# A transform and gated-MLP block: the last block of G kept on the chip, chunks ahead of products in the second, and one w_sp sum made in the last stage

## Chip, cores and metric

The kernel runs on one core of a Trainium2 chip. The metric is the device time of one execution in microseconds (us); the median of several executions is compared. All data are fp32 in DRAM at the start and the end.

## What is computed

```python
h = layernorm(x) * (1 + ca) + sa                        # x: [2048, 512]
x = x + ga * Re(DFT_seq(DFT_hid(h)))                    # Cr @ (h Wr') - Ci @ (h Wi')
h = layernorm(x) * (1 + cb) + sb
z = gelu(h @ w_in)                                      # [2048, 1792]
z1, z2 = z[:, :896], layernorm(z[:, 896:])
g = w_sp @ z2 + b_sp                                    # w_sp: [2048, 2048]
x = x + gb * ((z1 * g) @ w_out)
```

The six vectors sa, ca, ga, sb, cb, gb are silu(c) @ w_mod, cut into six pieces of 512; the text calls them vectors 0 to 5. Cr and Ci are the real and imaginary DFT matrices of the sequence (2048 x 2048), Wr and Wi those of the hidden axis. The kernel multiplies in the other order: first the sequence (G, from Cr, Ci and h), then the hidden axis (y, from G and Wr, Wi).

## The kernel before

**Products.** Each fp32 product is made as three matmuls of a reduced fp32 type: every operand is split into a high part (`hi`, a copy on ACT) and a rest (`lo`, a subtraction on DVE), and `matmul3` (L95) issues hi·hi, hi·lo and lo·hi. So for each block that PE multiplies, ACT makes one pass and DVE one or two (a transpose, and the rest).

**Slots and the order.** The program is one list of slots, each about 12 matmuls [128x128]·[128x512], and every other instruction is put at a slot by hand: `atd(n, f, ...)` runs `f` after the matmuls of slot n have been issued. All queues are in order: PE, ACT, DVE, POOL (stores, and small operations of the norms) and SP (loads). An instruction that waits holds back all that stands behind it on its engine.

**G stage, slots 0 to 121.** G is made in four row blocks of 512 rows.
- The first (t = 0) takes 32 slots (`mm_a`, L636) and all eight PSUM banks. While it runs, `load_first` (L572) loads four blocks of Cr and Ci for the products of t = 1 (roles 21, 11, 12, 22) and `turn_s` transposes them.
- Blocks t = 1, 2, 3 take 30 slots each, o..o+29 with o = 32, 62, 92: 14 slots of `s` units (`mm_s`, seven products of a Strassen-like scheme over sums of Cr and Ci blocks that `sum_f` makes, in the order 1, 5, 6, 2, 7, 3, 4), then 16 slots of `k` units (`mm_k`, plain chunks of Cr and Ci, two slots each). For every unit `turn_unit` transposes a chunk on DVE (the `k` units), `hi_unit` copies on ACT and `lo_unit` subtracts on DVE, two or three units ahead of its matmuls. After products 1, 5, 6 and 7 ACT copies PSUM banks (`mm_s`).
- Chunks come through a `stage` ring of two buffers: when one has been transposed, `block_done` loads the next but one.
- `out_k` (L708) stores the G of a block in DRAM (`g_d`): two ACT copies, two DVE sums and four stores of 256 KB a half.

**Modulation.** Vectors 2, 3, 4 are made by `load_mod`, `sum_mod` (four weighted sums on DVE), `split_mod`, and `spread_mod` (two matmuls with a matrix of ones). Vectors 0, 1 and 5 are made as columns: for each of four pieces a transpose (L184) and a product (L336) on DVE and a sum on ACT. Vector 5 then goes through DRAM (`store_mod`, `read_mod`).

**w_sp sums.** The spatial product, too, is made of products over sums of w_sp's quadrants. Four sums are made ahead of it: `load_s` loads four pieces of 128 x 512 (two loads of 512 KB), `sum_s` makes two sums on DVE in each of two calls and POOL stores them (`s_d`, four stores of 256 KB). There are 16 such sets (r, g, b), five in the G and y stages, eleven in z1.

**y stage, slots 122 to 153.** For each of 16 tiles of 128 rows: `load_g` (512 KB from `g_d`, two buffers), `split_g`, `seed_y` (ACT puts x into a PSUM bank), two slots of `mm_y` (j = 0, 1: real, imaginary), then `post_y` (ACT copy, store, statistics on DVE and POOL), `norm_y` (ACT) and `post_h` (two DVE operations, a store of h2).

**Then** come z1 (N2, h2 read back, loads `stage<-h_d`, the first half of w_in), z2, the spatial product gw (N4) and the output product.

Of the kernel before, what the change touches and what calls it, by code (L numbers as in the profile page):

```python
# [19 lines left out]
def fnet_gmlp_kernel(  # L20
# [531 lines left out]
    order_b = {}
    for t in range(1, NQ):
        more = t < NQ - 1
        names = ([("s", t + 1, 21), ("s", t + 1, 11), ("s", t + 1, 12)] if more else []) + \
            [("k", t, 0), ("k", t, 1), ("k", t, 2)] + ([("s", t + 1, 22)] if more else []) + [("k", t, 3)]
        for k in names:
            order_b[k] = 8 + len(order_b)
# [1009 lines left out]
```

## Time and profile before

| | us |
|---|---|
| runs before | 958.56, 960.98, 962.49 |
| median | 960.98 |
| profiled execution | 963.18 |
| its span, first to last instruction | 961.4 |
| granted TensorE clock, mean | 0.993 |

The profile gives times of the one profiled execution; 1.8 us of it lie outside the span. A stretch is found again by the stages: row block 0 of G until about 100 us, blocks 1 to 3 from 100.5, 184.6 and 270.5, y from 354, z1 from 449, z2 from 528, gw from 617, the output product from 905 us. PE runs the same kind of matmul nearly all the time, so a stretch in which PE waits shows as one with fewer matmuls.

### The profile page before, as it was taken

The page shows a single profiled execution, that of the slowest core. Times are in us where ns is not written, and L with a number is a line of the kernel's source. Part 1 is how long each engine was busy: PE and PEld are TensorE (multiplying, and loading weights), DVE is VectorE, ACT ScalarE, POOL GpSimd, SP SyncE. Part 2 cuts the span into 40 slices and gives each one's busy share as a digit, 9 for nine tenths or more (in the row PEclk, how much of TensorE's full clock was granted, in tenths as well). Part 3 has the DMA queues.
Part 4 walks back from the last instruction along what each step waited for, and adds up shares of the span by engine and source line. Part 5 has one row for each costly group of instructions (what it writes and reads, how often), then busy time and mean ns, then how long its engine had stood idle before and what let it go on. Part 6 is the DMA issues. An engine that isn't in the chain of part 4 may idle for free.

```text
span 961.4 us, 12161 instructions
## 1 busy us (share of the span) xinstructions
PE 932.5 (97%) x4086; PEld 769.7 (80%) x4086; DVE 747.7 (78%) x1021; ACT 434.7 (45%) x694; POOL 165.5 (17%) x333
## 2 busy tenths in 40 slices
PE   9989999999999998999979999999999999999998
PEld 6768887887878886787758999888888888888886
DVE  7789787998779864978767678888688679785882
ACT  3584543452254353554638355635544344432221
POOL 1330000100120113753333255400000000000000
PEclk9999999999999999999989999999999999999999
DMA  9997299759955739995996789664555355833541
GB/s 205 221 230 163 95 205 205 175 160 234 228 122 120 231 120 314 319 268 177 271 339 246 240 243 281 186 160 117 141 127 121 88 132 126 213 90 120 202 156 59
DMA packets 273743, 179.10 MB, mean 186 GB/s; under 512 B 135376, under 2 KB 240080, under 8 KB 273552
## 3 DMA queue, kind: packets, MB, share of 16 engines
q1 hardware_dynamic: 257136, 131.90, 57.1%
q0 software_dynamic: 13552, 43.81, 11.9%
q10 hardware_dynamic: 2992, 2.62, 1.1%
q8 instruction: 32, 0.52, 0.2%
q14 instruction: 31, 0.25, 0.1%
HBM read 133.17 MB, written 45.10 MB: 185 GB/s over the span
## 4 chain that ended last, share of the span: by engine, by line
PE 65%; DMA 11%; issue 9%; DVE 8%; POOL 4%; SPq 3%; ACT 1%; ACTq 0%; POOLq 0%; DVEq 0%
PE gw L98 9%; PE gw L99 9%; PE gw L97 9%; PE z2p L98 3%; PE z2p L97 3%; PE z2p L99 3%; PE op L97 3%; PE op L98 3%; PE op L99 3%; SPq L162 2%; DMA stage<-in_A_dft_seq_im_dram 2%; PE gs_c L98 2%; PE gs_c L97 2%; PE gs_c L99 2%; PE gp L98 2%
## 5 line engine op out<-in xcount | busy, mean ns | idle before, releaser
L98 PE MATMUL gw<-al,bh 128*128 128x512 f32 x400 | 155.9, 390 | 0.8 <-DVE al L270 0.8
L97 PE MATMUL gw<-ah,bh 128*128 128x512 f32 x400 | 155.6, 389 | 0.0
L99 PE MATMUL gw<-ah,bl 128*128 128x512 f32 x400 | 155.6, 389 | 0.0
L270 DVE TENSOR_TENSOR al<-t,ah 128x512 fp32r<-128x512 f32 x136 | 92.6, 686 | 60.2 <-PE gw L98 44.8
L263 ACT ACTIVATE ah<-t 128x512 fp32r<-128x512 f32 x136 | 84.7, 625 | 101.3 <-PE gw L99 56.1
L98 PEld LDWEIGHTS gw<-al,bh 128*128 128x128 f32 x400 | 75.1, 188 | 17.0 <-DVE al L270 1.6
L97 PEld LDWEIGHTS gw<-ah,bh 128*128 128x128 f32 x400 | 75.1, 188 | 15.8
L99 PEld LDWEIGHTS gw<-ah,bl 128*128 128x128 f32 x400 | 75.1, 188 | 15.5
L228 DVE STREAM_TRANSPOSE t<-stage 128x1024 f32<-128x1024 f32 x56 | 69.4, 1239 | 0.0
L1049 ACT ACTIVATE bh<-z 128x512 fp32r<-128x512 f32 (+1 forms) x56 | 32.8, 586 | 62.3 <-PE gw L98 62.3
L619 DVE TENSOR_TENSOR pl<-f,ph 128x1024 fp32r<-128x1024 f32 x42 | 50.8, 1212 | 12.8 <-ACT ph L615 12.6
L615 ACT ACTIVATE ph<-f 128x1024 fp32r<-128x1024 f32 x42 | 44.3, 1057 | 30.9 <-PE gs_c L99 8.9
L543 DVE STREAM_TRANSPOSE tp<-stage 128x1024 f32<-128x1024 f32 x36 | 44.5, 1235 | 16.9 <-DMA stage<-in_A_dft_seq_im_dram 11.5
L98 PE MATMUL gs_c<-pl,hh 128*128 128x512 f32 x144 | 56.2, 390 | 0.6 <-DVE pl L619 0.6
L97 PE MATMUL yp<-hth,gh 128*128 128x512 f32 x128 | 51.0, 398 | 5.3 <-ACT yp L812 5.3
L99 PE MATMUL gs_c<-ph,hl 128*128 128x512 f32 x144 | 56.1, 389 | 0.0
L97 PE MATMUL gs_c<-ph,hh 128*128 128x512 f32 x144 | 56.0, 389 | 0.0
L615 ACT ACTIVATE ph<-tp 128x1024 fp32r<-128x1024 f32 x35 | 36.9, 1054 | 37.2 <-DVE tp L543 16.6
L1027 POOL DMA_DIRECT2D s_d<-sj x64 | 35.4, 553 | 104.1 <-DVE sj L1019 53.4
L99 PE MATMUL yp<-hth,gl 128*128 128x512 f32 x128 | 50.6, 395 | 0.0
L98 PE MATMUL yp<-htl,gh 128*128 128x512 f32 x128 | 50.5, 394 | 0.0
L98 PE MATMUL z2p<-wil,ah 128*128 128x448 f32 x128 | 46.7, 365 | 0.0
(270 smaller groups left out, 2227.7 us busy)
## 6 DMA issues: line engine op xcount, KB each, us to landing
sj<-in_B_w_sp_dram SPq DMA_DIRECT2D x32, 512.0 KB, 7.0
s_d<-sj POOLq DMA_DIRECT2D x64, 256.0 KB, 5.5
stage<-s_d SPq DMA_DIRECT2D x128, 128.0 KB, 2.9
stage<-in_A_dft_seq_re_dram SPq DMA_DIRECT2D x52, 256.0 KB, 5.6
stage<-in_A_dft_seq_im_dram SPq DMA_DIRECT2D x52, 256.0 KB, 6.6
stage<-in_B_w_sp_dram SPq DMA_DIRECT2D x96, 128.0 KB, 3.2
gr<-g_d SPq DMA_DIRECT2D x16, 512.0 KB, 7.3
stage<-h_d SPq DMA_DIRECT2D x32, 256.0 KB, 6.6
```

The source lines that it names most:

```text
L97: nc.tensor.matmul(acc, ah, bh, start=first, stop=False, skip_group_check=go_on)
L98: nc.tensor.matmul(acc, ah, bl, start=False, stop=False, skip_group_check=go_on)
L99: nc.tensor.matmul(acc, al, bh, start=False, stop=last, skip_group_check=go_on)
L162: engs[q % len(engs)].dma_start(tile_[32 * q:32 * q + 32, :, s0:s1], v[q][:, :, s0:s1])
L228: nc.vector.transpose(t.rearrange("p r (b i) -> p r b i", i=32), st[:, :, :, 16 * k:16 * k + 32])
L263: nc.scalar.activation(AH[n], source(n), AF.Copy)
L270: nc.vector.tensor_tensor(AL[n], source(n), AH[n].bitcast(F32), op=ALU.subtract)
L543: nc.vector.transpose(dst.rearrange("p k (b i) -> p k b i", i=32), st[:, :, 64 * m:64 * m + 64].rearrange("p b (k i) -> p k b i", k=2))
L615: nc.scalar.activation(pair_of(PH, u, "ph"), source_unit(u), AF.Copy)
L619: nc.vector.tensor_tensor(pair_of(PL, u, "pl"), source_unit(u), PH[u].bitcast(F32), op=ALU.subtract)
L1027: nc.gpsimd.dma_start(s_d[m, r, g][b * P:(b + 1) * P, :], a)
L1049: nc.scalar.activation(BH[p, k][:, :w], b_of(p, k), AF.Copy)
```

## The change

- **Last row block of G.** `out_last` takes the place of `out_k` for t = 3: hi and lo of G are made from PSUM into SBUF tiles (ACT copies, DVE sums and subtractions), and `g_d[3]` is neither stored nor loaded. The y stage takes the tiles of this block first (order `YORD`), j = 0 for its four tiles and then j = 1; so these four end in successive slots. The buffers `gh` and `gl` become one ring of five. z1 takes the row blocks in the same order (`TS`).
- **Second row block (t = 1).** Four chunks (8 slots) come ahead of the products; `keep_p` copies their four banks to `UM[1]`. After products 1 and 5 DVE subtracts these from PSUM where ACT copied. The loads and transposes of the first `s` blocks, and the sums 5 and 7, come later.
- **Modulation.** Vector 5 is made like 2, 3, 4, ACT copying it from PSUM. The columns of 1 and 0 move from t = 1 to t = 2. Vectors 2, 4 and 3 are made earlier. `turn_ht` of the real part moves eight slots ahead.
- **w_sp sums.** A set is three pieces and three sums. The fourth, `sum_s4`, is made in gw from a quadrant of w_sp and the second sum: eight times two loads of 512 KB, one DVE subtraction [128x1024] and a store of 512 KB. The sets are placed anew: five in G, the others from YE+14.

```diff
+    TS = (NQ - 1, *range(NQ - 1))
     src = [quad((cr, ci)[j], 0, g) for g in range(NQ) for j in range(2)]
+    CHUNKS = {1: (("k", 1, 0), ("k", 1, 1), ("s", 2, 21), ("s", 2, 11), ("s", 2, 12), ("k", 1, 2), ("k", 1, 3), ("s", 2, 22)),
+              2: (("s", 3, 21), ("s", 3, 11), ("s", 3, 12), ("k", 2, 0), ("k", 2, 1), ("k", 2, 2), ("s", 3, 22), ("k", 2, 3)),
+              3: (("k", 3, 0), ("k", 3, 1), ("k", 3, 2), ("k", 3, 3))}
+    order_b = {}
     for t in range(1, NQ):
-        if t < NQ - 1:
-            src += [quad(cr, t + 1, 3), quad(cr, t + 1, 2), quad(ci, t + 1, 2)]
-        src += [quad(cr, t, 0), quad(cr, t, 1), quad(ci, t, 0)]
-        if t < NQ - 1:
-            src.append(quad(ci, t + 1, 3))
-        src.append(quad(ci, t, 1))
+        for kind, t_, i in CHUNKS[t]:
+            order_b[kind, t_, i] = len(src)
+            src.append(quad((cr, ci)[i // 2], t_, i % 2) if kind == "k" else
...
+        if j == 5:
+            mods[5] = cpool.tile([P, D], F32, tag="mod5", bufs=1, name="mod5")
+            nc.scalar.activation(mods[5], ps, AF.Copy)
+            return
...
+        first = 4 if t == 1 else 0
+        units += [("k", t, i) for i in range(first)] + [("s", t, i) for i in range(14)] + \
+            [("k", t, i) for i in range(first, 8)]
...
-        return {"c11": 0, "u": 2 if t % 2 else 4, "v": 4 if t % 2 else 2, "c22": 6}[role]
+        return {"c11": 0, "u": 2 if t == 3 else 4, "v": 4 if t == 3 else 2, "c22": 6}[role]
...
+                if t == 1:
+                    nc.vector.tensor_tensor(C["u", f], C["c11", f], UM[t][:, f, :], op=ALU.subtract)
+                else:
+                    nc.scalar.activation(C["u", f], C["c11", f], AF.Copy)
...
+                um = UM[t][:, 2 + f, :]
+                if t == 1:
+                    nc.vector.tensor_tensor(um, C["v", f], um, op=ALU.subtract)
+                else:
+                    nc.scalar.activation(um, C["v", f], AF.Copy)
...
+    def keep_p():
+
+        for f in range(2):
+            nc.scalar.activation(UM[1][:, f, :], C["c11", f], AF.Copy)
+        for f in range(2):
+            nc.scalar.activation(UM[1][:, 2 + f, :], C["v", f], AF.Copy)
...
+        if fresh and s == 7:
+            UM[t] = outs.tile([P, 4, D], F32, tag="um", bufs=1, name=f"um{t}")
+            keep_p()
...
+    def ring(name, dtype=F32R):
+        return yp[0].tile([P, 2, D], dtype, tag="gt", bufs=5, name=name)
+
+    def out_last(j):
+
+        def lo(dst, src, hi):
+            nc.vector.tensor_tensor(dst, src, hi.bitcast(F32), op=ALU.subtract)
+
+        t = NQ - 1
+        um = UM[t][:, 2 * j:2 * j + 2, :]
+        if j == 0:
+            hs, ls = [[ring(f"gt{m}0"), None] for m in "hl"]
+        else:
+            both_ = [blocks.tile([P, 4, D], F32R, tag="stage", bufs=2, name=f"gt{m}1") for m in "hl"]
+            hs, ls = [[b[:, 2 * e:2 * e + 2, :] for e in range(2)] for b in both_]
+        for f in range(2):
+            nc.scalar.activation(hs[0][:, f, :], C["u" if j else "c11", f], AF.Copy)
+        for f in range(2):
+            nc.vector.tensor_tensor(um[:, f, :], C["c22" if j else "v", f], um[:, f, :], op=ALU.add)
+        for f in range(2):
+            lo(ls[0][:, f, :], C["u" if j else "c11", f], hs[0][:, f, :])
+        if j == 0:
+            hs[1], ls[1] = [ring(f"gt{m}1") for m in "hl"]
+        nc.scalar.activation(hs[1], um, AF.Copy)
+        lo(ls[1], um, hs[1])
+        for e in range(2):
+            for f in range(2):
+                GT[4 * j + 2 * e + f] = hs[e][:, f, :], ls[e][:, f, :]
...
-        YP[m] = bank(4 + m % 4, f"yp{m}")
+        i = YORD.index(m)
+        YP[m] = bank((0, 1, 4, 5)[i] if i < 4 else (6, 7, 4, 5)[i % 4], f"yp{m}")
         nc.scalar.activation(YP[m], X.pop(("r", m)), AF.Copy)
...
+            gh, gl = [g[:, m % 4 * P:m % 4 * P + P] for g in GT[c_]] if m // 4 == NQ - 1 else \
+                (GH[m][:, c_, :], GL[m][:, c_, :])
+            matmul3(YP[m], gh, gl, ht_hi[j, k], ht_lo[j, k], False, c_ == 7, True)
...
+        nc.sync.dma_start(t[:, 0], w_sp[o:o + P, g * Q:(g + 1) * Q])
+        v = w_sp.rearrange("r (j c) -> r j c", j=2)[S // 2 + o:S // 2 + o + P]
+        nc.sync.dma_start(t[:, 1:], v[:, :, g * Q:(g + 1) * Q])
...
-            nc.vector.tensor_tensor(a12, a12, a11, op=ALU.subtract)
-            done = (2, a11), (4, a12)
+            done = (2, a11),
...
+    def load_s4(r, g, h):
+
+        t = S4[r, g, h] = spre[-1].tile([P, 2, 2, Q], F32, tag="hz", bufs=2, name=f"s4_{r}{g}{h}")
+        rows_ = slice(2 * h * P, 2 * (h + 1) * P)
+        for i, a in enumerate((quad(w_sp, r, 2 + g), s_d[2, r, g])):
+            nc.sync.dma_start(t[:, i], a[rows_].rearrange("(b p) c -> p b c", p=P))
+
+    def sum_s4(r, g, h):
+        t = S4.pop((r, g, h))
+        nc.vector.tensor_tensor(t[:, 0], t[:, 0], t[:, 1], op=ALU.subtract)
+        nc.gpsimd.dma_start(s_d[4, r, g][2 * h * P:2 * (h + 1) * P].rearrange("(b p) c -> p b c", p=P), t[:, 0])
...
-    for role, l, n, m in ((21, 8, 12, 14), (11, 10, 16, 18), (12, 15, 20, 22), (22, 19, 24, 26)):
+    for role, l, n, m in ((21, 12, 16, 18), (11, 14, 20, 22), (12, 24, 31, 33), (22, 33.5, 35, 36)):
...
-                     (29, (lo_v, 6), (sum_f, 1, 5, 1)), (30, (out_a, 0, (2, 3)), (sum_f, 1, 7, 0)),
-                     (31, (sum_f, 1, 7, 1), (lo_v4,)), (32, (out_a, 1, (0, 1))), (34, (out_a, 1, (2, 3)))):
+    for n, *todo in ((23, (change_f,), (sum_v, 5)), (24, (hi_v, 5)), (25, (lo_v, 5), (sum_v, 7), (sum_v, 6)),
+                     (26, (hi_v, 7), (sum_v, 4)), (27, (lo_v, 7), (hi_v, 6)), (28, (out_a, 0, (0, 1))),
+                     (30, (lo_v, 6), (out_a, 0, (2, 3)), (hi_v4,)), (32, (lo_v4,)), (34, (out_a, 1, (0, 1))),
+                     (36, (out_a, 1, (2, 3))), (37, (sum_f, 1, 5, 0)), (38, (sum_f, 1, 5, 1)),
+                     (39, (sum_f, 1, 7, 0)), (40, (sum_f, 1, 7, 1))):
...
+            atd(o + ((22, 29) if t == 1 else (21, 29))[j], *((out_last, j) if t == NQ - 1 else (out_k, t, j)))
...
+            for role, n, m in (((21, 13, 14), (11, 15.5, 16.5), (12, 17.5, 18.5), (22, 24, 25)) if t == 1 else
+                               ((21, 3, 5), (11, 7.5, 8.5), (12, 9.5, 10.5), (22, 21, 23))):
...
-    for j, l, n in ((1, 39, 46), (0, 43, 51), (5, 89, 93)):
+    for j, l, n in ((1, 66, 73), (0, 67, 77)):
...
-    for j, l, ns, m, plus_one in ((2, 50, (55, 56, 57), 60, False), (4, 75, (78, 79, 80), 84, True),
-                                  (3, 81, (85, 86, 87), 89.5, False)):
+    atd(82, scale_columns)
+    for j, l, ns, m, k, plus_one in ((2, 37, (40, 41, 42), 44, 6, False), (4, 46, (56, 57, 58), 60, 3, True),
+                                     (3, 58.5, (63, 64, 65), 66, 7, False), (5, 78, (82, 83, 85), 87, 0, False)):
...
-        n, d = ((62, 6), (68, 6), (118, 5), (121, 6), (126, 5))[i] if i < 5 else             (YE + (4, 5, 15, 25, 27, 29, 31, 33, 35, 37, 39)[i - 5], (4, 8, 6, 4, 4, 4, 4, 4, 4, 4, 3)[i - 5])
+        atd(m, spread_mod, j, k, plus_one)
+    early = ((43.5, 53), (85.5, 89), (86.5, 91), (109, 113), (117, 120))
+    early += tuple((YE + c, YE + c + 4) for c in (14, 17, 20, 23, 27, 29, 31, 33, 35, 37, 38))
+    for (n, m), u in zip(early, [(r, g, b) for g in range(2) for b in range(4) for r in range(2)]):
         atd(n, load_s, *u)
-        atd(n + d, sum_s, *u, True)
-        atd(n + d + 1, sum_s, *u, False)
+        atd(m, sum_s, *u, True)
+        atd(m + 1, sum_s, *u, False)
...
-    for n, *todo in ((-2, (load_ht, 0)), (6, (turn_ht, 0, 0)), (7, (turn_ht, 0, 1)), (8, (scale_w0, 0), (turn_ht, 0, 2), (turn_ht, 0, 3)),
+    for n, *todo in ((-6, (load_ht, 0)), (-3, (turn_ht, 0, 0)), (-2, (turn_ht, 0, 1)), (-1, (turn_ht, 0, 2)), (0, (turn_ht, 0, 3)), (8, (scale_w0, 0)),
...
+    for i, m in enumerate(YORD):
+        n, e = (Y0 + i, Y0 + 4 + i) if i < 4 else (Y0 + 2 * i, Y0 + 2 * i + 1)
+        if i > 3:
+            atd(n - 3, split_g, m)
+        if 4 <= i + 2 < 16:
+            atd(n - 2.5 if i > 3 else o + 17 + i - 2, load_g, YORD[i + 2])
+        atd(n - 2 if i > 3 else o + 27 + i // 2, seed_y, m)
+        if i + 2 < 16:
+            atd(n - 1.5 if i > 3 else o + 27 + i // 2, load_xr, YORD[i + 2])
+        atd(e + 1, post_y, m)
+        w = 2.5 if i < 4 else 3.5
+        atd(e + w if i < 14 else YE + 2, norm_y, m)
+        atd(e + w + 1 if i < 14 else YE + 3, post_h, m)
...
-    for m in range(16):
-        for j in range(2):
-            mm_y(m, j)
-            run(("d", n))
-            run(("d", n + 0.5))
-            n += 1
+    for m, j in [(m, j) for j in range(2) for m in YORD[:4]] + [(m, j) for m in YORD[4:] for j in range(2)]:
...
+    for n, u in zip((4, 8, 12, 15, 49, 52, 55, 58), [(r, g, h) for g in range(2) for h in range(2) for r in range(2)]):
+        at(N4 + n - 4, load_s4, *u)
+        at(N4 + n, sum_s4, *u)
```

More of the change, by code (lines that the diff above doesn't have):

```diff
@@ L82, in fnet_gmlp_kernel @@
     g_d = [dram.tile([8, P, Q], F32, name=f"g_d{t}") for t in range(NQ)]
-    row_d = {j: dram.tile([1, D], F32, name=f"row_d{j}") for j in (2, 3, 4)}
+    row_d = {j: dram.tile([1, D], F32, name=f"row_d{j}") for j in (2, 3, 4, 5)}
     x2_d = [dram.tile([Q, D], F32, name=f"x2_d{t}") for t in range(NQ)]
@@ L147, in fnet_gmlp_kernel @@
     N2 = 4 * len(src)
-    src += h2_d + h2_d
+    src += [h2_d[t] for t in TS] + h2_d
     FORMS = (1, 2, 6, 7, 4, 5, 3)
@@ L317, in fnet_gmlp_kernel @@
     WB, WT = {}, {}
-    COL = {j: cpool.tile([P, ND], F32, name=f"col{j}") for j in (0, 1, 2, 5)}
+    COL = {j: cpool.tile([P, ND], F32, name=f"col{j}") for j in range(3)}
     def load_row():
@@ L525, in fnet_gmlp_kernel @@
     ORD = (1, 5, 6, 2, 7, 3, 4)
+    YORD = [4 * t + i for t in TS for i in range(4)]
     D1 = 8 * NQ
@@ L531, in fnet_gmlp_kernel @@
     for t in range(1, NQ):
-        units += [("s", t, i) for i in range(14)]
-        units += [("k", t, i) for i in range(8)]
+        first = 4 if t == 1 else 0
+        units += [("k", t, i) for i in range(first)] + [("s", t, i) for i in range(14)] + \
+            [("k", t, i) for i in range(first, 8)]
+    at_unit = {u: n for n, u in enumerate(units)}
     PH, PL, TP, FT = {}, {}, {}, {}
@@ L547, in block_done @@
         stage.pop(b)
-        if b + 2 < NC:
+        if b + 2 < NC and b + 2 not in (order_b["k", 3, 0], order_b["k", 3, 1]):
             load(b + 2)
     SB = {}
[L552 to L558, printed above, removed]
     def turn_s(t, role, m):
@@ L674, in mm_s @@
         acc = {1: "c11", 2: "c11", 5: "v", 3: "v", 6: "u", 7: "u", 4: "u"}[p]
-        if m == 0 and p in (1, 5):
+        fresh = p in (1, 5) and t > 1
+        if m == 0 and fresh:
             for f in range(2):
                 C[acc, f] = bank(set_of(t, acc) + f, f"gs{t}_{acc}_{f}")
-        u = 16 + 22 * (t - 1) + i
+        if t not in UM and p == 5:
+            UM[t] = outs.tile([P, 4, D], F32, tag="um", bufs=1, name=f"um{t}")
+        u = at_unit["s", t, i]
         ph, pl = PH.pop(u), PL.pop(u)
@@ L682, in mm_s @@
                 matmul3(C[acc, f], *form_v(p, 2 * m + c_, f), ph[:, c_, :], pl[:, c_, :],
-                        p in (1, 5) and m == 0 and c_ == 0, m == 1 and c_ == 1, p not in (1, 5))
+                        fresh and m == 0 and c_ == 0, m == 1 and c_ == 1, not fresh)
         if m == 0:
@@ L1005, in load_s @@
         if spre:
-            SJ[r, g, b] = spre[-1].tile([P, 4, Q], F32, tag="sj", bufs=2, name=f"sj{r}{g}{b}")
-        elif not yp:
-            SJ[r, g, b] = raw([P, 4, Q], f"sj{r}{g}{b}")
-        else:
-            SJ[r, g, b] = blocks.tile([P, 4, Q], F32, tag="stage", bufs=2, name=f"sj{r}{g}{b}")
-        for i in range(2):
-            v = w_sp.rearrange("(i r) (j c) -> i r j c", i=2, j=2)[i]
-            o = r * Q + b * P
-            nc.sync.dma_start(SJ[r, g, b][:, 2 * i:2 * i + 2], v[o:o + P][:, :, g * Q:(g + 1) * Q])
+            t = spre[-1].tile([P, 3, Q], F32, tag="sj", bufs=2, name=f"sj{r}{g}{b}")
+        elif n_now[0] not in (85, 86):
+            t = raw([P, 3, Q], f"sj{r}{g}{b}")
+        else:
+            t = blocks.tile([P, 3, Q], F32, tag="stage", bufs=2, name=f"sj{r}{g}{b}")
+        SJ[r, g, b] = t
+        o = r * Q + b * P
+        nc.sync.dma_start(t[:, 0], w_sp[o:o + P, g * Q:(g + 1) * Q])
+        v = w_sp.rearrange("r (j c) -> r j c", j=2)[S // 2 + o:S // 2 + o + P]
+        nc.sync.dma_start(t[:, 1:], v[:, :, g * Q:(g + 1) * Q])
     def sum_s(r, g, b, first):
-        a11, a12, a21, a22 = [SJ[r, g, b][:, i] for i in range(4)]
+        a11, a21, a22 = [SJ[r, g, b][:, i] for i in range(3)]
         if first:
```

86 lines of the change are left out of this document (30 added, 56 removed).

## The prediction

> **What bounds the kernel now.** I read the shares of the engines first, then windows over each stage, then the timelines and the chain of waits at the places where matmuls are missing.
>
> ```profile
> PE 932.5 (97%) x4086; PEld 769.7 (80%) x4086; DVE 747.7 (78%) x1021; ACT 434.7 (45%) x694; POOL 165.5 (17%) x333
> ```
>
> TensorE (PE) is busy for 97% of the span, so the kernel is bound by its matmuls, whose number the change hardly alters. All that it can win are the places where PE waits. The next fence is the table by windows: start and end, then busy time and count of PE, weight loads, DVE, ACT and POOL, granted clock, DMA share and GB/s.
>
> ```profile
> core 0: us, PE busy (x) PEld busy (x) DVE busy (x) ACT busy (x) POOL busy (x), PEclk, DMA share, GB/s
> 40.00:50.00 10.00, 10.00 (x46) 8.29 (x45) 3.99 (x6) 5.10 (x11) 4.08 (x14) 1.00 1.16 224
> 50.00:60.00 10.00, 6.84 (x24) 5.18 (x23) 8.38 (x9) 8.15 (x16) 2.75 (x10) 0.83 1.24 229
> 160.00:180.00 20.00, 18.14 (x79) 14.32 (x78) 17.04 (x22) 6.25 (x11) 1.92 (x4) 1.00 0.63 151
> 220.00:230.00 10.00, 8.82 (x38) 6.61 (x37) 9.86 (x11) 3.18 (x3) 2.17 (x4) 1.00 0.93 226
> 270.00:290.00 20.00, 18.54 (x80) 14.34 (x79) 17.06 (x19) 12.78 (x22) 3.75 (x6) 1.00 0.36 86
> 370.00:390.00 20.00, 16.42 (x66) 13.04 (x65) 11.51 (x17) 7.26 (x10) 9.97 (x18) 0.91 1.07 320
> 430.00:440.00 10.00, 8.73 (x38) 6.89 (x38) 6.45 (x11) 3.11 (x5) 4.98 (x10) 1.00 1.02 312
> 450.00:470.00 20.00, 17.94 (x79) 14.20 (x78) 13.86 (x24) 12.53 (x22) 9.23 (x17) 1.00 0.79 262
> 490.00:510.00 20.00, 13.81 (x49) 10.63 (x50) 15.49 (x20) 10.22 (x19) 5.93 (x11) 0.83 1.08 334
> 100.50:184.60 84.10, 82.25 (x361) 67.40 (x361) 67.43 (x70) 37.72 (x56) 3.47 (x6) 1.00 0.80 175
> 184.60:270.50 85.90, 84.72 (x373) 69.50 (x372) 68.61 (x71) 32.26 (x39) 10.27 (x19) 1.00 0.82 202
> 270.50:354.00 83.50, 82.04 (x360) 66.92 (x359) 71.54 (x83) 39.97 (x58) 9.75 (x17) 1.00 0.48 131
> 617.00:905.00 288.00, 287.75 (x1268) 237.92 (x1269) 228.37 (x335) 118.68 (x208) 7.09 (x15) 1.00 0.52 132
> ```
>
> The first row is a stretch without a wait: 46 matmuls in 10 us, one per 0.217 us. By that, a row with fewer has lost the missing matmuls times 0.217, clock included (a few records may be missing, so this leans high). At 50–60 us it is 22, so 4.8 us; at 160–180, 220–230 and 270–290 (starts and middles of the row blocks) 2.4, 1.7 and 2.2; in the y stage, 370–390 and 430–440, 5.2 and 1.7; in z1, 450–470 and 490–510, 2.4 and 8.9. Together 29.3 us is what an edit of order can reach. The last three stage rows are row blocks 1 to 3 of G (second to fourth); the gw stage, 617–905, has no loss to win.
>
> **The change part by part.**
>
> *First row block (50–60 us), −4.6.*
>
> ```profile
> 51.62 1.25 DVE L543 STREAM_TRANSPOSE f<-sb 128x1024 f32<-128x1024 f32 x1 [5.49 <-DMA sb<-in_A_dft_seq_re_dram]
> ```
>
> This DVE row shows the cause: the transpose of the first `s` block stood 5.49 us waiting for its load, and the lo split that PE needed stood behind it in DVE's queue. The transposes move from slots 12 and 14 to 16 and 18 (a slot, about 12 matmuls, is 2.7 us), some 11 us later, while the load is issued 4 slots later too. The load may be late there again. But at slot 16 the split of the unit that starts then stands ahead of the transpose, and the next unit is wanted two slots, 5.4 us, later; a wait of 4 us is covered there, as it isn't at slot 12. I leave 0.2 of the 4.8. Bounds: 0 won (at a DMA share of 1.16–1.24 the load is later than that cover) and 4.8.
>
> [...]
>
> *Row blocks 1 to 3, +1.0.* PE needs 30 slots of 2.72, 81.7 us, for a block; the question is DVE.
>
> ```profile
> L619 DVE TENSOR_TENSOR pl<-f,ph 128x1024 fp32r<-128x1024 f32 x13 | 15.8, 1214 | 7.4 <-ACT ph L615 7.4
> L543 DVE STREAM_TRANSPOSE tp<-stage 128x1024 f32<-128x1024 f32 x8 | 9.9, 1242 | 7.9 <-DMA stage<-in_A_dft_seq_im_dram 5.4 <-DMA stage<-in_A_dft_seq_re_dram 2.5
> ...
> L584 DVE TENSOR_TENSOR f<-f,f 128x1024 f32<-128x1024 f32 x8 | 9.7, 1218 | 0.0
> L336 DVE TENSOR_TENSOR wt<-wt,crow 128x512 f32<-128x512 f32 x8 | 5.5, 692 | 0.3
> L184 DVE STREAM_TRANSPOSE wt<-wb 128x512 f32<-128x512 f32 x8 | 5.5, 686 | 0.0
> L315 DVE SCALAR_TENSOR_TENSOR wm<-wm,sc 128x512 f32<-128x512 f32 x3 | 2.2, 750 | 0.1
> L713 DVE TENSOR_TENSOR um<-gs_v,um 128x512 f32<-128x512 f32 x2 | 1.2, 663 | 0.0
> ```
>
> These are DVE's groups in row block 1 (busy, mean ns, idle before). Block 1 loses the columns of vectors 1 and 0 (8 × 0.686 + 8 × 0.692 = 11.0, with their two small ends 11.4) and four chunk transposes that move ahead of it (3.7 of them inside the window). It gains vector 4 (3.4: four weighted sums of 0.75 at most, a split of 0.7), one set of three w_sp sums (2.0), the four subtractions from PSUM (4 × 0.66, L713 being such an operation: 2.7), four sums 5/7 of `sum_f` (4 × 1.218 = 4.9), three block transposes (3.7) and the last lo of v4 (1.4). So 67.4 becomes 70.4 of 81.7. Of the subtractions two pairs stand at the ends of slots 41 and 43 and must wait for PE to finish that product; behind each the lo split of a later unit is queued. In the old order ACT made these copies. PE has two units prepared ahead, so a pair costs between 0 and a whole slot, 2.7; nearest is a wait of about 0.7 each. `keep_p` puts four copies more on ACT, busy 37.7 of 84.1: hidden, or 4 × 0.6 if a hi split stands behind them at the moment. With the reload of chunks (7.9 us of waits for `stage` in the second row) still there, I take 2.9 where it was 2.4.
>
> Block 2 loses two sets of w_sp sums (8 × 0.69 = 5.5) and gains five operations of the new sets (3.4), the columns (11.0) and three transposes of `turn_ht` (2.1): 68.6 becomes about 79.6. That is 97% of 81.7, and DVE waits as well. Block 3 gives up vector 5's columns at its start (2.2 lost there). I take 4.4 for both where it was 3.9, so the blocks together +1.0. Bounds: −6.3 (all stalls of the blocks gone) and +23.5 (rival 3).
>
> *y stage, −5.5.*
>
> ```profile
> 375.90 1.28 ACTq L845 DMA_DIRECT2D wraw<-in_B_w_in_dram  x3
> 377.29 0.81 ACT L121 ACTIVATE h<-x,nmry,rsy 128x512 f32<-128x512 f32 x1 [8.49 <-issue]
> ```
>
> ```profile
> 361.51 14.37 DMA gr<-g_d
> ...
> 478.82 12.88 DMA stage<-h_d
> ```
>
> The second fence is from the chain of waits: a load of G took 14.37 us, and the norm on ACT stood 8.49 us. Eight stores and four loads of G leave the stage's start (8 × 256 KB + 4 × 512 KB = 4 MB, at 320 GB/s some 13 us of DMA), G's last row block is there when y begins, and the next `load_g` starts well ahead of its use. For it ACT makes 4 copies and DVE 4 subtractions more at slot 113 and 121, in place of the two `out_k` calls. Of 5.2 I leave 0.5; of 1.7 at 430–440, where a DMA share of 1.02 remains, 0.9. 6.9 − 1.4 = 5.5. Bounds: 0 and 6.9 won; a loss is rival 2.
>
> *z1, −6.8.*
>
> ```profile
> 492.02 2.37 DVE L877 STREAM_TRANSPOSE hz<-stage 128x1024 f32<-128x1024 f32 x2 [8.10 <-DMA stage<-h_d]
> ```
> ```profile
> 465.06 0.82 ACT L121 ACTIVATE h<-x,nmry,rsy 128x512 f32<-128x512 f32 x1 [3.97 <-DMA h_d<-h]
> ```
>
> The last gap is DVE waiting 8.10 us for a block of h2, whose load (the chain, 478.82) took 12.88 us in a stage with DMA share 1.08. The fourth w_sp sum leaves: 16 DVE operations and 4 MB of stores in all, 1 MB of stores and the loads of a quadrant beside each set in this stretch, at 334 GB/s 3 us and more. The sets start at YE+14 where two stood at YE+4 and 5. The block's load, the same size, can then land some 3 us sooner, or more as its neighbours leave too; I leave 3 of the 8.9 and 1.5 of the 2.4, together 4.5 of 11.3. Bounds: 0 and 11.3.
>
> *Others.* Vector 5 on PE: two matmuls, +0.45. The fourth sums in the gw stage: eight DVE operations of 1.22 (as L584, the same size) are 9.8 on a DVE that is idle 59.6 of 288 us, with 16 loads and 8 stores at DMA share 0.52: hidden, so 0. If that cover goes, each holds back a lo split by up to 1.2, so 0 to +9.8; I take 0, since the rows of that stage show PE without a gap.
>
> Sum: −4.6 + 1.0 − 5.5 − 6.8 + 0.45 = −15.5. The profiled execution took 963.2 us (span 961.4 and 1.8 around it), so 947.7 of its kind; it stood 2.2 above the median 960.98, which gives 945.5.
>
> **Rivals.**
>
> *1. The z1 stall persists* (the load waits on the store of h2, not on the queue). For it: the row 465.06, a norm waiting for a store `h_d<-h`; the order of tiles leaves the last pair as late as ever. Against: 12.88 us for 256 KB is a share of a full queue. Without the 6.8: 952.
>
> *2. The burst of the first four y tiles.* Their ends come one slot apart, where two slots were usual.
>
> ```profile
> 387.18 0.54 POOL L823 DMA_DIRECT2D x_d<-x  x1
> 387.80 0.55 POOL L109 TENSOR_SCALAR mvy<-mvy 128x1 f32<-128x1 f32 x1
> 388.43 0.90 POOL L110 TENSOR_TENSOR rsy<-mvy,mhalf 128x1 f32<-128x1 f32 x1
> 389.44 0.32 POOL L117 TENSOR_SCALAR nmry<-mvy,rsy 128x1 f32<-128x1 f32 x1
> ```
>
> POOL needs for one tile about 2.3 us here and a store of h2 at 0.54 more, so 2.9; four are 11.6 against four slots, 10.9. With 1.3 more for each where one of two h2 buffers waits for its store (an estimate, half of POOL's own time), 4.2 each, they are 16.8. The last is then 5.9 late, less the 2.2 us by which a bank is free ahead: a gap of 3.7 and 1.5 of half clock: 945.5 + 5.2 = 951. Against: POOL is busy half the time at 370–390 and those rows contain other stores, which go.
>
> [...]
>
> *3. The other side: DVE becomes the bound in row blocks 1 and 2.* If its waits stay beside the added work, block 2 needs 79.6 and the 17.3 us that DVE stood idle there (85.9 − 68.6), 96.9, 15.2 over 81.7; block 1 needs 70.4 + 16.7 (84.1 − 67.4) and 4 for the two slot-end waits, 91.1, 9.4 over. Less the 4.1 lost there now, +20.5, and some 3 for the clock in the new gaps (as at 50–60): +23.5 where I have +1, so 945.5 + 22.5 = 968. It outweighs the 16.5 won elsewhere once about 80% of the two blocks' 34 us of waits remain. For it: waits for `stage` are DMA, and do not shrink because DVE has more to do.
>
> ```profile
> L543 DVE STREAM_TRANSPOSE tp<-stage 128x1024 f32<-128x1024 f32 x8 | 9.9, 1242 | 8.7 <-DMA stage<-in_A_dft_seq_im_dram 6.0 <-DMA stage<-in_A_dft_seq_re_dram 2.6
> ```
>
> Against: in block 1, 7.4 of the waits were for ACT's `ph`, DVE being ahead; a later DVE finds loads landed.
>
> *4. The change does not do what it says for time:* stalls only move, the loads being as many bytes in the stretch. Between 956 and 964.
>
> **How the numbers follow.** My forecast has 0.60 (range 937–952: about half of the three large terms, 16.9, too much or too little, cut off at rival 1), rival 1 0.13, rival 2 0.10, rival 4 0.10, rival 3 0.07. The likeliest gives 945.5. The range 934–958 takes in rivals 1 and 2 and the near part of 4; at its low end nearly all 29.3 us are gone (963.2 − 29.3 + 0.45 − 2.2 = 932). It leaves out rival 3 and the far part of 4. A measurement of this kernel tells from no change what is over 0.5%, 4.8 us: faster is below 956.2, the forecast with rivals 1 and 2, 0.82 after a hundredth goes to the middle; same 0.11; slower 0.07.
>
> **What would show it.** In the profile after: 50–60 us with 44 matmuls or more and no DVE wait of 5 us for `sb`; block 2 no longer than 86.5 us with DVE 79–80 busy in it (rival 3: over 92 us and DVE waits of 15 or more); 370–390 with some 88 matmuls (rival 2: a gap on a bank of `yp` with POOL's L110 ahead); the wait for `stage<-h_d` at z1 under 4 us (rival 1: still 8); gw's 288 us within 1. I would be wrong if DVE's added 11 us in block 2 met its waits, or if loads and not stores fill the queue in z1.

## The result, and the profile after

The changed kernel took 997.05 us (median of four runs, 995.26 to 998.91) against 959.77 before: ratio 1.0389, 95% interval 1.0347 to 1.0432. The forecast was 945.5. The table gives the time from the first matmul of each stage to that of the next, in the two profiled executions and in that of the changed kernel with one pad tile 32 bytes longer (the first experiment below). By these bounds gw runs from 607.9 to 881.3 us before; the stretch from 617 to 905 that the prediction took for it holds 24 us of the output product.

| us | before | after | after, with pad | forecast of the change |
|---|---|---|---|---|
| row block 0 | 93.2 | 93.4 | 88.2 | −4.6 |
| row blocks 1 to 3 | 253.8 | 283.6 | 261.9 | +1.0 |
| y | 95.3 | 89.7 | 88.3 | −5.5 |
| z1 | 80.2 | 79.7 | 78.9 | −6.8 |
| z2 | 77.8 | 77.8 | 77.8 | 0 |
| gw | 273.4 | 282.3 | 276.3 | 0 |
| out, to the end of the span | 80.1 | 82.1 | 79.8 | 0 |

The y stage went as forecast. Row blocks 1 to 3 grew by 30 us, and gw and the output product, which issue the same matmuls as before, by 11. The next two fences are the table by windows (PE, weight loads, DVE, ACT, POOL, clock, DMA share, GB/s) for row blocks 1 to 3 and for gw, before and after.

```profile
100.80:354.60 253.80, 249.30 (x1092) 204.09 (x1091) 208.09 (x223) 110.54 (x152) 23.95 (x43) 1.00 0.70 170
607.90:881.30 273.40, 272.64 (x1201) 225.07 (x1200) 220.27 (x323) 117.49 (x205) 10.82 (x23) 1.00 0.54 135
```

```profile
101.80:385.50 283.70, 259.62 (x1094) 210.33 (x1094) 219.63 (x241) 111.08 (x148) 20.66 (x38) 0.96 0.75 159
...
632.70:915.00 282.30, 280.38 (x1201) 225.51 (x1200) 226.33 (x327) 117.35 (x205) 15.01 (x28) 1.00 0.85 173
```

In gw PE is busy throughout in both, at clock 1.00, with 1201 matmuls; after, they take 8 us more. The DMA share went from 0.54 to 0.85, while the rate rose only from 135 to 173 GB/s: each transferred byte keeps the DMA engines busy longer. So two things changed, the pace of the matmuls and the time of the transfers, and two more views show them one by one. First PE's timeline in gw (start, duration), before and after:

```profile
700.22 0.39 PE L99 MATMUL gw<-ah,bl 128*128 128x512 f32 x1
700.45 0.39 PE L97 MATMUL gw<-ah,bh 128*128 128x512 f32 x1
700.67 0.39 PE L98 MATMUL gw<-al,bh 128*128 128x512 f32 x1
700.90 0.39 PE L99 MATMUL gw<-ah,bl 128*128 128x512 f32 x1
```

```profile
700.11 0.40 PE L97 MATMUL gw<-ah,bh 128*128 128x512 f32 x1
700.34 0.40 PE L98 MATMUL gw<-al,bh 128*128 128x512 f32 x1
700.58 0.40 PE L99 MATMUL gw<-ah,bl 128*128 128x512 f32 x1
700.81 0.40 PE L97 MATMUL gw<-ah,bh 128*128 128x512 f32 x1
```

The starts are 0.227 us apart before and 0.2333 after (0.70 for three). Then the DMA issues of the page (size, median us to landing), before and after:

```profile
stage<-s_d SPq DMA_DIRECT2D x128, 128.0 KB, 2.9
stage<-in_A_dft_seq_re_dram SPq DMA_DIRECT2D x52, 256.0 KB, 5.6
...
stage<-in_B_w_sp_dram SPq DMA_DIRECT2D x96, 128.0 KB, 3.2
```

```profile
stage<-s_d SPq DMA_DIRECT2D x128, 128.0 KB, 4.2
stage<-in_A_dft_seq_re_dram SPq DMA_DIRECT2D x52, 256.0 KB, 7.8
...
stage<-in_B_w_sp_dram SPq DMA_DIRECT2D x96, 128.0 KB, 4.8
```

These transfers land 39 to 50% later, though not every group did (`stage<-in_A_dft_seq_im_dram` went from 6.6 to 6.3). In the row blocks this makes DVE wait, and PE behind it; the largest wait on DVE and the largest gap on PE there, with the time idle in brackets:

```profile
122.16 1.25 DVE L538 STREAM_TRANSPOSE f<-sb 128x1024 f32<-128x1024 f32 x1 [14.87 <-DMA sb<-in_A_dft_seq_im_dram]
```

```profile
245.01 0.79 PE L98 MATMUL gs_u<-pl,hh 128*128 128x512 f32 x1 [6.44 <-DVE pl L607]
245.60 0.63 PE L99 MATMUL gs_u<-ph,hl 128*128 128x512 f32 x1
246.03 0.63 PE L97 MATMUL gs_u<-ph,hh 128*128 128x512 f32 x1
```

After the gap of 6.44 us the starts are 0.43 apart for a while, in place of 0.23: the granted clock is 0.5 (the half clock) from 241.6 to 248.5 us, and that costs on top.

What in the diff could slow a matmul and a load that it does not touch? The constant pool loses one tile of 16 bytes a partition, in a line that the diff above leaves out:

```diff
-    COL = {j: cpool.tile([P, ND], F32, name=f"col{j}") for j in (0, 1, 2, 5)}
+    COL = {j: cpool.tile([P, ND], F32, name=f"col{j}") for j in range(3)}
```

By the addresses that the built program gives its tiles, every pool behind it on the left side starts 32 bytes lower. Before, all working tiles but those of one small pool (`spool`, the same in both) start at multiples of 512 bytes in their partition; after, those of the left pools (`blocks`, `raws`, `pairs`, `hpa`, `hpb`, `zab` and others) start at 480 modulo 512, those of the right pools at 0 as before. Sorted by the addresses of their two operands, the matmuls 128x512 of the trace after that follow one another without a wait fall apart cleanly: 1871 with one operand on each side are 0.2333 us apart, 1728 with both on the same side 0.2271.

### The profile page after: what moved, and what is told of

Its sections match the earlier page's. It is cut to its first block, busy times and chain, and to the rows that moved or that the text cites. A ratio compares the mean times of both kernels' runs of the same rounds, so it can differ in the third digit from the quotient of the medians.

```text
span 997.1 us, 12127 instructions
## 1 busy us (share of the span) xinstructions
PE 952.3 (96%) x4088; PEld 775.8 (78%) x4088; DVE 746.4 (75%) x1016; ACT 433.1 (43%) x686; POOL 157.4 (16%) x312
## 4 chain that ended last, share of the span: by engine, by line
PE 65%; issue 13%; DMA 10%; DVE 6%; POOL 2%; SPq 2%; ACT 1%; ACTq 0%; DVEq 0%; POOLq 0%
PE gw L98 8%; PE gw L99 8%; PE gw L97 8%; DMA stage<-in_A_dft_seq_im_dram 3%; PE op L99 3%; PE op L97 3%; PE op L98 3%; PE z2p L98 3%; PE z2p L99 3%; PE z2p L97 3%; PE gp L98 2%; PE gp L99 2%; PE gp L97 2%; DMA stage<-h_d 2%; DVE pl L607 2%
## 5 line engine op out<-in xcount | busy, mean ns | idle before, releaser
L98 PE MATMUL gw<-al,bh 128*128 128x512 f32 x400 | 158.6, 396 | 1.9 <-DVE al L273 1.9
L99 PE MATMUL gw<-ah,bl 128*128 128x512 f32 x400 | 158.4, 396 | 0.0
L97 PE MATMUL gw<-ah,bh 128*128 128x512 f32 x400 | 158.4, 396 | 0.0
L99 PEld LDWEIGHTS gw<-ah,bl 128*128 128x128 f32 x400 | 75.2, 188 | 18.1
L1069 POOL DMA_DIRECT2D s_d<-sj x48 | 26.5, 552 | 141.7 <-DVE sj L1062 98.1
L99 PE MATMUL z2p<-wih,al 128*128 128x448 f32 x128 | 46.8, 366 | 0.0
L97 PE MATMUL z2p<-wih,ah 128*128 128x448 f32 x128 | 46.8, 365 | 0.0
L98 PE MATMUL gs_u<-pl,hh 128*128 128x512 f32 x72 | 30.7, 426 | 14.5 <-DVE pl L607 14.5
```

Source lines behind the costliest of these rows:

```text
L97: nc.tensor.matmul(acc, ah, bh, start=first, stop=False, skip_group_check=go_on)
L98: nc.tensor.matmul(acc, ah, bl, start=False, stop=False, skip_group_check=go_on)
L99: nc.tensor.matmul(acc, al, bh, start=False, stop=last, skip_group_check=go_on)
L1069: nc.gpsimd.dma_start(s_d[m, r, g][b * P:(b + 1) * P, :], a)
```

## The experiments

**1. The 32 bytes back, and taken from the kernel before.** Three kernels that differ from theirs by a pad alone, with the same instructions.

```diff
 after_pad, from after:
-    cpool.tile([P, LINES // 8], F32, name="lines")
+    cpool.tile([P, LINES // 4], F32, name="lines")
 before_shift, from before:
-    cpool.tile([P, LINES // 8], F32, name="lines")
 before_shift_all, from before, also:
-    edge.tile([P, (-32 % 512) // 4], F32, name="edge")
+    edge.tile([P, (-64 % 512) // 4], F32, name="edge")
```

> The changed kernel with one pad tile 32 bytes longer, so that the tiles of the left pools start again at a multiple of 64 bytes as they did before the change; no instruction differs. In the changed kernel 1871 matmuls whose two operands start differently modulo 64 stand 0.2333 us apart, the others 0.227. Theory A (the 32 bytes are the cause of most: they slow matmuls and also the loads into left-pool tiles): all matmuls 0.227 apart, DMA share in the gw stage back from 0.9 to about 0.55, row blocks 1 to 3 near 255 us instead of 284, time 943 to 958. Theory B (the loads are late because of where the change puts them; the 32 bytes cost matmul rhythm alone): 12 us less, 983 to 988, with the gaps of 5 to 6 us in the row blocks still there. Theory C (the rhythm has another cause): 997.

> The kernel before without its 32-byte pad tile, so that the left pools lie 32 bytes off a multiple of 64, as in the changed kernel; no instruction differs. Theory A: matmuls with unlike operands 0.2333 apart (+12 us) and loads into left-pool tiles slower, so that DVE waits for them in the row blocks: 978 to 997. Theory B: +12 alone, 970 to 974. Theory C: 960.

> The kernel before with the left and the right pools both 32 bytes off a multiple of 64, so that both operands of every matmul agree modulo 64; no instruction differs. If unlike operands are what slows a matmul, all are 0.227 apart. Theory A adds that loads into every pool are slow: 968 to 990, with a DMA share in the gw stage near 0.95. Theory B: 960, DMA share 0.52.

Against the kernel before: with the pad 0.9979 (0.9955 to 1.0003), 959.17 us, where the change without it stands at 1.0389. The kernel before without its pad: 1.036 (1.0334 to 1.0386), 995.78 us. With the pad, row blocks 1 to 3 and gw read so in the table by windows:

```profile
95.60:357.50 261.90, 253.16 (x1094) 206.72 (x1093) 216.97 (x236) 111.14 (x148) 20.66 (x38) 0.99 0.70 170
602.50:878.80 276.30, 274.16 (x1202) 226.28 (x1201) 225.64 (x325) 117.18 (x205) 14.46 (x27) 0.99 0.68 175
```

In gw the DMA share is 0.68, where the changed kernel needs 0.85 for about the same rate (175 and 173 GB/s).

So 32 bytes make 35 to 38 us in either kernel, and the change itself, left to its edits, makes next to nothing. The places differ: in the kernel before, the loss is 11 us in row block 0, 10 in row blocks 1 to 3 and 11 in gw; in the changed one 5, 22 and 6. That the two sums come out so near each other is in part chance.

Theory A is right about the pad; its time for `after_pad` (943 to 958) is just missed, since the edits win less than forecast. B, that the places in the order make the loads late, is refuted for most of the loss. `before_shift_all` came out slower still (1.0407, 1.0373 to 1.0440; 999.6 us where theory A had 968 to 990), and its matmuls with one operand on each side are still 0.2333 apart: there the left tiles lie at 480 and the right ones at 32, alike modulo 64 but not modulo 128. So it did not take the two costs apart.

**2. The two costs apart, and the boundary.**

```diff
 all_480:
-    edge.tile([P, (-32 % 512) // 4], F32, name="edge")
-    cpool.tile([P, LINES // 8], F32, name="lines")
+    edge.tile([P, 512 // 4], F32, name="edge")
 all_64 (all_256: -288 and 72):
+    edge.tile([P, (-96 % 512) // 4], F32, name="edge")
+    cpool.tile([P, 24], F32, name="lines")
```

> The kernel before with the left and the right pools both 32 bytes lower, all working tiles at 480 modulo 512; no instruction differs. It parts the two costs of the 32 bytes. Theory A (matmuls are slowed when the starts of their two operands differ, loads when their tile starts off a boundary, each by itself): matmuls 0.227 apart again, loads as slow as with the left pools alone shifted, so the 36 us shrink by 12 to about 983. Rival (the starts must be multiples of 64 for a matmul to be quick): 0.2333 for all or half of them, 995 or more. [...]

> The kernel before with all working tiles at 64 modulo 512 in place of 0. If the boundary for the loads is 32 or 64 bytes: 960, DMA share in the gw stage 0.52. [...]

> The kernel before with all working tiles at 256 modulo 512. If the boundary is 256 bytes or less: 960. If it is 512: 975 to 985.

Measured: all tiles at 480, 1.0309 (1.0276 to 1.0341), 991.7 us; all at 64, 1.0274 (1.0228 to 1.0320), 986.3 us, not the 960 of a boundary of 32 or 64 bytes; all at 256, 0.9998 (0.9973 to 1.0022). In each fence below stands one stretch of gw, 700 to 800 us, in the table by windows: `before`, `before_shift`, `all_480`, `all_64`, `all_256`.

```profile
700.00:800.00 100.00, 100.00 (x443) 82.81 (x442) 79.37 (x114) 44.57 (x79) 0.00 (x0) 1.00 0.51 114
```
```profile
700.00:800.00 100.00, 100.00 (x430) 80.63 (x429) 73.31 (x104) 45.71 (x82) 1.64 (x3) 1.00 0.72 114
```
```profile
700.00:800.00 100.00, 100.00 (x442) 82.77 (x442) 76.13 (x108) 45.49 (x81) 2.18 (x4) 1.00 0.71 116
```
```profile
700.00:800.00 100.00, 100.00 (x442) 82.79 (x442) 74.37 (x106) 47.10 (x85) 1.64 (x3) 1.00 0.73 114
```
```profile
700.00:800.00 100.00, 100.00 (x443) 82.81 (x442) 79.24 (x114) 43.94 (x78) 0.00 (x0) 1.00 0.52 116
```

Read the PE count and the DMA share. With like operands PE makes 442 or 443 matmuls in 100 us, wherever they lie; with unlike ones 430. The DMA share for the same 114 to 116 GB/s is 0.51 to 0.52 at 0 and 256, and 0.71 to 0.73 at 480 and 64. These are two effects. With all pools off the boundary the loads cost about 3% by themselves, at a normal pace of the matmuls; with the left pools alone, as in the change, they were not measured apart from the pace. The rival that a start must be a multiple of 64 for a quick matmul falls with the 442 matmuls of `all_480`; the loads are slow there (DMA share 0.71) beside matmuls at the quick pace, so they do not need slowed ones. That slower operations of DVE or ACT are behind it falls as well: their mean times in the seven traces at 0, 64, 256 and 480 agree (the lo split of 128x512 takes 680 to 682 ns in each).

The pace adds some 1800 × 0.0062 = 11 us at most; `before_shift_all`, which has both costs, is 0.0098 of the time or 9 us above `all_480`. Against `before_shift`, `all_480` gains only 4 us, not the 12 of theory A. By the stages of the traces the pace does come back, in gw (277.4 us against 284.8) and the output product (80.1 against 82.3), but the y stage is longer (99.1 against 92.7). Its loads go to tiles of a right pool, which of these two kernels is off the boundary in `all_480` alone; that this is the reason was not shown.

The packets of the DMA engines show what the transfers pay. One of 256 bytes, of which the kernel moves 122,880, takes 18.1 ns in the trace before and 26.7 in `before_shift`; one of 512 bytes 39.4 and 46.0, one of 2 KB 100.9 and 105.6, one of 4 KB (these are in POOL's queue) 168.4 and 174.1. So each packet costs some 5 to 9 ns more in all four sizes, and the smallest pieces lose by far the largest share, 48% against 3 to 17.

For the loads 256 is as good as 0 in this stretch (DMA share 0.52 and 0.51) and 64 as bad as 480 (0.73 and 0.71). So the boundary is above 64 bytes and at most 256; 128 was not tried.

**3. The late transposes alone, on the kernel before.**

```diff
-    for role, l, n, m in ((21, 8, 12, 14), (11, 10, 16, 18), (12, 15, 20, 22), (22, 19, 24, 26)):
+    for role, l, n, m in ((21, 12, 16, 18), (11, 14, 20, 21), (12, 18.5, 23, 24), (22, 21.5, 26, 27)):
```

> The kernel before with one part of the change alone: the first s blocks are loaded and transposed four slots later (transposes at slots 16 to 27 in place of 12 to 26). Theory: the stall at 55.75 us goes, as in the changed kernel with the pad: -4.5 to -5, ratio 0.995. Rival (the load is as late at slot 16 and stalls there): 0.999 to 1.002.

0.9951 (0.9932 to 0.9971), 5.5 us less. The gap at 55.75 us is gone from the trace, as from that of the padded kernel, and row block 0 takes 88.8 us in place of 93.2. This term was right.

**4. What held back the padded kernel.** Its largest stalls on PE are at 156.9 and 222 us (4.3 us each, with the half clock behind them), 489.7 (8.7) and 654 (4.0). Three moves, alone and together:

```diff
 pad_mods:
-    for j, l, n in ((1, 66, 73), (0, 67, 77)):
+    for j, l, n in ((1, 72, 75), (0, 73, 78)):
-    atd(82, scale_columns)
-    for j, l, ns, m, k, plus_one in ((2, 37, (40, 41, 42), 44, 6, False), (4, 46, (56, 57, 58), 60, 3, True),
-                                     (3, 58.5, (63, 64, 65), 66, 7, False), (5, 78, (82, 83, 85), 87, 0, False)):
+    atd(83, scale_columns)
+    for j, l, ns, m, k, plus_one in ((2, 37, (40, 41, 42), 44, 6, False), (4, 51, (58, 59, 60), 62, 3, True),
+                                     (3, 61, (66, 67, 68), 69, 7, False), (5, 79.5, (83, 84, 85), 87, 0, False)):
 pad_wi:
-                     (8, (load_wi, 1, 2), (load, N2 // 4 + 3)),
+                     (8, (load, N2 // 4 + 3)),
...
-                     (12, (turn_z, 3)), (14, (sum_z, 1)),
+                     (12, (turn_z, 3), (load_wi, 1, 0)), (13, (load_wi, 1, 2)), (14, (sum_z, 1)),
 pad_s4:
-    for n, u in zip((4, 8, 12, 15, 49, 52, 55, 58), [(r, g, h) for g in range(2) for h in range(2) for r in range(2)]):
-        at(N4 + n - 4, load_s4, *u)
+    for n, u in zip((6, 12, 18, 24, 49, 53, 57, 61), [(r, g, h) for g in range(2) for h in range(2) for r in range(2)]):
+        at(N4 + n - (6 if n < 30 else 4), load_s4, *u)
```

> The changed kernel with the pad, and the loads of the modulation moved behind the first two chunk loads of their row block (vector 4 from slot 46 to 51, columns 1 and 0 from 66 and 67 to 72 and 73, vector 3 from 58.5 to 61, vector 5 from 78 to 79.5; the sums with them). Theory: the gaps at 156.9 and 222 us (4.3 and 4.3 with their clock) come from chunk loads that share the queue with these: both under 1.5, 5 to 7 us less than the changed kernel with the pad. Rival (DVE is full in block 2 whatever the loads do): the gap at 222 only moves to a later slot, 0 to 3 less.

> The changed kernel with the pad, and the two loads of w_in for the second half of z1 (1.8 MB) moved from slots N2+7 and N2+8, ahead of the loads of h2, to N2+12 and N2+13 behind them. Theory (these loads fill the queue in front of h2's, not the w_sp sums as the prediction had it): the z1 gap at 489.7 us, 8.7 with its clock, shrinks to 1 to 3, 5 to 7 less. Rival (the stores of z1 by POOL, 2.7 MB at the same time, fill it): 0 to 2 less.

> The changed kernel with the pad, and the first four of the fourth w_sp sums six slots apart in place of three to four, each with six slots between its loads and its sum. Theory: the gap at 654 us (4.0 with its clock) is DVE waiting 1.9 us for a load of such a sum and 1.25 for a load of w_out behind its store: 3 to 4 less. Rival: the load of w_out is late by itself, 1 less.

> The three moves together on the changed kernel with the pad: if they add, 13 to 17 us less than it, 943 to 947 on its scale of 959; if the stalls only move on, within 5 of it.

`pad_mods`: 0.9999 (0.9976 to 1.0021), nothing won, as its rival had it. The gap at 157 is gone; in its place stand 4.1 at 226 to 231 and 5.1 at 253 to 258. The stalls moved on. `pad_wi`: 0.9931 (0.9907 to 0.9955), 4.4 us less than the padded kernel where 5 to 7 were expected, and the gap at 489.7 is gone (two of about 1 us stay behind it). `pad_s4`: 0.9946 (0.9927 to 0.9965), 3.2 us less, and no gap left in gw. The gap's cause was what the DVE timeline of the padded kernel shows: a sum and then `wor` each wait for a load, with the `al` split for gw queued behind:

```profile
650.17 1.23 DVE L1082 TENSOR_TENSOR s<-s 128x1024 f32<-128x1024 f32 x1 [1.93 <-DMA s<-s_d]
...
652.64 0.69 DVE L1175 TENSOR_TENSOR wor<-wor,mod 128x512 f32<-128x512 f32 x1 [1.25 <-DMA wor<-in_B_w_out_dram]
```

`pad_three`: 0.9919 (0.9897 to 0.9942), 7 us less than the padded kernel and not 13 to 17: the two moves that help add up, the third adds nothing.

**5. The two moves that helped, what z1 waited for, and block 2.** The last two kernels leave out the loads or the work of two columns; they serve for the time alone.

```diff
 pad_two: after_pad with pad_wi's and pad_s4's edits
 before_two: before_late with pad_wi's edit
 no_col_loads, from pad_two, in load_columns:
-        load_block(WB[j], quad(w_mod, 0, j))
+        nc.gpsimd.memset(WB[j], 0.5)
 no_col_work, from pad_two, in weigh_column and sum_column:
-        WT[j, k] = temp(f"wt{j}_{k}")
-        squares(WT[j, k], WB[j], k)
-        nc.vector.tensor_tensor(WT[j, k], WT[j, k], WB["c"], op=ALU.mult)
+        if k == 3:
+            nc.gpsimd.tensor_scalar(COL[j], WB[j][:, 0, :ND], 1.0, None, op0=ALU.mult)
...
-        w = WT.pop((j, k))
-        nc.scalar.activation(w, w, AF.Copy, accum_out=COL[j][:, k:k + 1])
```

> The changed kernel with the pad, the w_in loads behind those of h2, and the first fourth sums six slots apart, without the moves of the modulation that did not help. The two moves gave 4.4 and 3.2 alone; if they add: 951 to 952, ratio 0.990; if one stall takes the other's place, 954 to 956.

> The kernel before with the late transposes of the first s blocks and with the w_in loads behind those of h2; nothing else of the change. The stalls at 55.75 (5.0) and 495 to 504 us (9.5 with the clock) go: 961 less 5 less 6 to 9, so 947 to 951, ratio 0.985 to 0.989. If the stores of w_sp's sums, which the kernel before has in this stretch, fill the queue (as the prediction had it), only 1 to 3 of the 9: 953 to 955.

> As pad_two, with the loads for the columns of vectors 1 and 0 in row block 2 left out (2 MB; a constant is written in their place), their DVE work kept. Theory L (chunk loads that share the queue make the stalls at 221 and 254 us): both gone or under 1 us, 4 to 6 less than pad_two. Theory D (DVE has too much to do in block 2): 0 to 1 less.

> As pad_two, with the DVE and ACT work of these columns left out (11 us of DVE; a few values are copied in their place), their loads kept. Theory L: 0 to 2 less than pad_two. Theory D: 4 to 6 less, the stalls at 221 and 254 us gone.

`pad_two` is the version that beats both kernels, if by less than 1%: 952.12 us, 0.9921 (0.9893 to 0.9949), the same as `pad_three`. `before_two` gave nothing (0.9997, 0.9981 to 1.0013), where 947 to 951 us were expected. The w_in loads behind h2's, which freed z1 in the changed kernel, shrink the gap here from 7.9 to 5.5 us (with the clock) and open one of 5.1 at 504, where ACT now waits for them:

```profile
499.05 0.95 ACT L854 ACTIVATE wih<-wraw 128x896 fp32r<-128x896 f32 x1 [5.28 <-DMA wraw<-in_B_w_in_dram]
```

So in z1 neither traffic explains the stall by itself. With the w_sp stores still there (kernel before) moving the w_in loads shortens the wait without a gain in time; with those stores gone and the w_in loads in place (padded kernel) the wait is as long as ever:

```profile
486.72 2.37 DVE L919 STREAM_TRANSPOSE hz<-stage 128x1024 f32<-128x1024 f32 x2 [8.63 <-DMA stage<-h_d]
```

With both edits it is gone. The two kernels differ in more than these stores, so what share each traffic had stays open.

For block 2, here is the wait of DVE for its first chunk, in `pad_two`, `no_col_loads` and `no_col_work`:

```profile
215.60 1.25 DVE L538 STREAM_TRANSPOSE tp<-stage 128x1024 f32<-128x1024 f32 x1 [3.14 <-DMA stage<-in_A_dft_seq_re_dram]
```
```profile
215.59 1.25 DVE L538 STREAM_TRANSPOSE tp<-stage 128x1024 f32<-128x1024 f32 x1 [1.03 <-DMA stage<-in_A_dft_seq_re_dram]
```
```profile
219.28 1.25 DVE L536 STREAM_TRANSPOSE tp<-stage 128x1024 f32<-128x1024 f32 x1 [3.92 <-DMA stage<-in_A_dft_seq_re_dram]
```

Without the columns' loads it falls from 3.1 to 1.0 us, since the chunk now takes 6.8 us from the issue of its first piece to the landing of its last, where it took 8.9. PE's stall at 219 falls from 4.2 us to two of 0.7 and 0.8; without the columns' work the wait stays, and so does the stall (3.6). The smaller gap at 252 (1.6) is the other way round: it goes without the work and stays without the loads. So by the gaps L is right for the larger and D for the smaller.

The time does not follow the gaps. The medians (949.77, 0.9891 with 0.9860 to 0.9921; 947.00, 0.9864 with 0.9830 to 0.9898) are 2 and 5 us under that of `pad_two`, which looks like D, but the intervals overlap its own. In the profiled executions block 2 takes 88.5, 86.3 and 86.5 us; block 1, in which the three do the same, takes 85.3, 87.2 and 87.5, and the three row blocks together 259.5, 260.6 and 259.8. So either edit wins some 2 us in block 2, which is no more than executions differ by elsewhere. What makes the stalls at 156 and 275 (1.2 to 3.7 us in all three) was not tried here.

## Why the prediction was wrong

The step that failed is the first one: "All that it can win are the places where PE waits". It took the pace of a matmul and the landing times of the loads as given, and the sum has no term for where tiles lie. The shorter `COL` and the pad tile "lines" beside it stood in the code; neither was asked about. Where the sum has nothing, the 32 bytes made 38 of the 52 us by which the forecast is off: 997 against 959 with the pad, by loads that keep the DMA engines busy longer and by matmuls 0.2333 us apart in place of 0.2271. The rival on the other side, DVE bound in blocks 1 and 2 at 968, has the place of most of the loss right but not the mechanism: DVE did stand waiting there, for loads that had become slower.

The other 14 us lie in the row blocks, z1 and gw; row block 0 and y won a little more than forecast. They are read in the column with the pad.

- **Row block 0, −4.6:** −5.0. Right in mechanism and size, as `before_late` shows alone.
- **y, −5.5:** −7.0. Right in sign and somewhat larger. Two losses of 0.4 and 0.5 us are all that is left in the stage; rival 2, the burst of four tiles, did not come. Its gap of 3.7 us with 1.5 of half clock is a term that no run shows; what the trace before shows in this stage is a gap of 3.58 us, at 380.07, with 3.4 us at the half clock (380.6 to 384.0 us), of which 1.7 are lost.
- **Row blocks, +1.0:** +8.1, most of it in blocks 1 (84.6 to 87.8 us) and 2 (84.3 to 87.9, where the sign was 86.5 at most). The DVE busy time grew by 9 us over the three blocks (208.09 before, 216.97 with the pad) where the working gave about 14 for blocks 1 and 2, so the work was not under-counted. The step that failed is the argument "a later DVE finds loads landed". Over the three blocks DVE waits 16.6 us for loads before and 21.4 with the pad, in these groups:

```profile
L543 DVE STREAM_TRANSPOSE tp<-stage 128x1024 f32<-128x1024 f32 x24 | 29.7, 1239 | 16.6 <-DMA stage<-in_A_dft_seq_im_dram 11.3 <-DMA stage<-in_A_dft_seq_re_dram 5.2
```
```profile
L538 DVE STREAM_TRANSPOSE tp<-stage 128x1024 f32<-128x1024 f32 x21 | 26.0, 1238 | 11.6 <-DMA stage<-in_A_dft_seq_im_dram 8.5 <-DMA stage<-in_A_dft_seq_re_dram 3.0
L538 DVE STREAM_TRANSPOSE f<-sb 128x1024 f32<-128x1024 f32 x3 | 3.7, 1228 | 9.8 <-DMA sb<-in_A_dft_seq_im_dram 9.8
```

The text asked where each DVE operation goes, not what each moved load stands in front of. For one stall, that of block 2's first chunk, experiment 5 shows the columns' loads in front of the chunk. The cause of the rest of the 7 us stays open: the stalls moved when single loads were moved (`pad_mods`), and no edit of the padded kernel made the row blocks shorter than 259.5.
- **z1, −6.8:** −1.3. "The block's load can then land some 3 us sooner" is refuted: the load that DVE waits for took 12.9 us before and 15.7 with the pad. With the w_in loads moved as well, no such load of this stretch took more than 9.2, and the stage 72.8 (`pad_wi`). Rival 1 (the stall persists) held for the result, but not for its reason, a wait on the store of h2: the stall went when other loads made room.
- **gw, 0:** +2.9. The sums' own time was hidden as forecast; their loads' latency was not, since DVE waits in order (1.93 and 1.25 us one behind the other, in the fence of experiment 4). With those loads issued earlier the stage takes 272.0 (`pad_s4`). The stated bound (0 to +9.8) held it. In the unpadded kernel the stage grew by 8.9, of which 6 are the pace and the loads.
- **Vector 5 on PE, +0.45,** is too small to be told apart.

One reading was a little off without changing the outcome. The 46 matmuls of the row 40–50 us include those that the window's edges cut; the starts are 0.227 us apart, not 0.217. So the 29.3 us of stalls were some 5% more.
